# A fused attention and routing kernel: v loaded by heads, two units of filler work moved, and the first k on GpSimd's queue

## The chip, the core and the metric

The kernel runs on one core of a Trainium2 chip. The metric is the device time of one execution in microseconds. Before the change it is 891.77 us, the median of three runs (891.57 to 892.58). One further execution was profiled, and all rows below are of that one.

## What is computed

Two blocks follow each other. The first is an attention without softmax, on four batches of four heads, 1088 positions and 32 values for each position. Each vector of q and k is sent through two small matrices S1 and S2 (8 by 32), and its features are the 64 products of the two results:

```python
def phi(x):
    a = np.einsum('rd,bhsd->bhsr', S1, x)
    b = np.einsum('rd,bhsd->bhsr', S2, x)
    return np.einsum('bhsi,bhsj->bhsij', a, b).reshape(*x.shape[:-1], r * r)
kv = np.einsum('bhsf,bhsd->bhfd', phi(k), v)
z = np.sum(phi(k), axis=2)
num = np.einsum('bhsf,bhfd->bhsd', phi(q), kv)
den = np.einsum('bhsf,bhf->bhs', phi(q), z)[..., None] + 1e-06
```

The result, 4352 rows of 128, is the input x of a dense mixture of eight experts. Logits are `x @ w_gate`; eight rounds of row and column normalisation make weights of them; the output is the sum over the experts of the weight times `relu(x @ w1[e]) @ w2[e]`, with w1 128 by 1024 and w2 1024 by 128.

## The kernel before, in words

Almost all of the arithmetic is the experts' matrix products in float32 on TensorE. The kernel is written so that TensorE can begin them as early as possible. Batch 0 of the attention is worked out first, by itself. From then on there are two streams. One is the attention of batches 1 to 3 and the routing (`attention`, `routing`), which is short on TensorE and waits a great deal for VectorE, ScalarE and DMAs. The other is "filler": products of experts 0 and 1 on the rows of x that are ready, cut into small steps by the generator `steps` (lines L735 for the first product and L797 for the second). Where the attention says `yield n`, the driver calls `fill(n)`, which puts n units of filler on TensorE at that place of the program. TensorE works strictly in the order of the program, so a unit that stands behind a waiting attention product waits too. After the routing the driver drains what is left of the filler, and `weighted` computes everything else (L1076 and L1226, until the end).

The order on TensorE, VectorE and ScalarE is, for the first part, the order of the text. The order on SP, the engine that issues nearly all DMAs, and on GpSimd is made by a scheduler that places each instruction by its own estimate of when it can go. SP issues in that order and waits at the head of it. A DMA also waits for the DMA that is eight places before it on the same queue, since eight semaphores are used in turn.

The names that the steps below touch:

- `load_k`, `load_q`, `load_v` (L169 to L189): one batch of k, q or v into the on-chip memory. k and q come as one DMA of 128 partitions each. v has its positions spread so that partition 32 c + s holds eight positions of block c of row s, for all four heads; it is loaded as four DMAs of 32 partitions (one block c each, all heads) of 128 KB, and two small ones of 32 partitions.
- `projections` (L217 to L225): S1 and S2, which arrive as 64-bit numbers, made into float32 on VectorE (L34 to L47), transposed (`st`, L222) and spread by heads into `wd` (L223). `wd` and the transposed keys `kT` (L269) are what the first real product of TensorE needs (L280).
- `keys_ab`, `keys_products`, `keys_sums` (L280, L295, L310): features of k and their sums with v. `keys_sums(b)` is the reader of v.
- `queries_ab`, `repeat_a`, `repeat_b` (L396 to L423): for batches 1 to 3 the features of q are made through DRAM. Two small products per position (`qab`) are stored to `qa` and `qb` in DRAM, repeated on the way, and read back as `ph` (four DMAs of 288 KB) and `rb` (one of 1152 KB). `times(b, c)` (L430) multiplies them on VectorE, and `tops(b, c)` (L439) multiplies the product with the sums of the keys on TensorE.
- the warming products of ones (L119), six rounds, which keep TensorE at work until the first keys are there.
- the memsets at the beginning, on GpSimd but for three.
- `settle`, `chores_of` (L1327, L1018): inside `weighted`, work on the kept sums of experts 0 and 1: the load of a row of weights (`pk`) and the products with it, put into a list that is worked off at spare places.

Of the kernel before, what the change touches and what calls it, by code (L numbers as in the profile page):

```python
# [10 lines left out]
F32 = mybir.dt.float32  # L11
# [40 lines left out]
def kernel(  # L52
# [12 lines left out]
    nc = tc.nc  # L65
    P = nc.NUM_PARTITIONS
# [36 lines left out]
    for n, (s, queue) in enumerate(((S1, nc.sync), (S2, nc.scalar))):  # L103
        queue.dma_start(out=raw[:, n], in_=s.bitcast(U32).unsqueeze(0).to_broadcast([P // R, R, words * D]))

    def starts(tile_, c0, blocks):

        for c in blocks:
            nc.gpsimd.memset(tile_[32 * c:32 * (c + 1), c0:c0 + 1], 1.0)


    ones = consts.tile([P, P], F32, name="ones")
    nc.gpsimd.memset(ones, 1.0)
    warm = [aps.tile([P, 512], F32, tag="a", name="a") for _ in range(2)]
    for _ in range(6):
        for r in range(2):
            for c in range(2):
                rows, cols = slice(64 * r, 64 * (r + 1)), slice(64 * c, 64 * (c + 1))
                nc.tensor.matmul(warm[r][cols, 0:256], ones[rows, cols], ones[rows, 0:1].to_broadcast([64, 256]),  # L119
                                 start=True, stop=True, tile_position=(64 * r, 64 * c))  # L120
# [28 lines left out]
    kvs = []  # L149
    for i in range(2):  # L150
        kvs.append(consts.tile([P, 2, 2, D + 1], F32, name=f"kvs{i}"))
        nc.gpsimd.memset(kvs[i], 0.0)

    eps = consts.tile([P, 3, H], F32, name="eps")
    nc.gpsimd.memset(eps, 1e-6 / P)

    v_slots = []
    for i in range(2):
        t = wk.tile([P, H + 1, NT + 1, D], F32, name=f"v{i}", bufs=1)
        nc.vector.memset(t[:, H], 1.0)  # L160
        nc.gpsimd.memset(t[H2:P, 0:H, NT], 0.0)
        v_slots.append(t)

    ab = wk.tile([P, 2, NT + 1, H * R], F32, name="ab", bufs=1)
    nc.gpsimd.memset(ab[H2:P, :, NT], 0.0)

    loaded, pools = {}, []

    def load_k(b):  # L169
        kx = ld.tile([P, SA, D], F32, tag="k", name="kx", bufs=1)  # L170
        nc.sync.dma_start(out=kx, in_=k[b].rearrange("h (s a) d -> (h s) a d", a=SA))
        loaded["k", b] = kx

    def load_q(b, lo=0, hi=SA):
        if not lo:
# [3 lines left out]

    def load_v(b):  # L180
        vx, o = v_slots[b % 2], v[b].offset
        for c in range(4):
            nc.sync.dma_start(
                out=vx[32 * c:32 * (c + 1), 0:H, 0:NT, :].rearrange("p h t d -> p h (t d)"),
                in_=AP(tensor=v.tensor, offset=o + NT * D * c, ap=[[SA * D, 32], [S * D, H], [1, NT * D]]))
        for c in range(2):
            nc.sync.dma_start(
                out=vx[32 * c:32 * (c + 1), 0:H, NT, :],
                in_=AP(tensor=v.tensor, offset=o + (4 * NT + c) * D, ap=[[SA * D, 32], [S * D, H], [1, D]]))  # L189

    load_k(0)
    load_q(0, 0, 8)
    load_v(0)
    load_q(0, 8)
# [23 lines left out]
    def projections():  # L218
        flat = raw.rearrange("p n d -> p (n d)")
        s12 = f64_to_f32(nc, consts, flat, (P, 2 * D)) if words == 2 else flat.bitcast(F32)  # L220
        st = consts.tile([P, 2, 32], F32, name="st")
        nc.vector.transpose(out=st.rearrange("p n r -> p (n r)"), in_=s12)  # L222
        nc.vector.tensor_tensor(wd, st[:, :, 0:R].unsqueeze(2).to_broadcast([P, 2, H, R]),  # L223
                                own.unsqueeze(1).unsqueeze(3).to_broadcast([P, 2, H, R]), op=Alu.mult)
        return st  # L225

# [257 lines left out]
    def attention(b):  # L484


        follows = b + 1 < B
        keys_sums(b)
        times(b, 0)
        yield 1.7 if b == 1 else 2  # L490
        keys_kept(b)
        times(b, 1)
        tops(b, 0)
        if b == 1:
            transpose_q(2)
        yield 1.4
        times(b, 2)
        over(b, 0)
        tops(b, 1)
        if b == 1:  # L500
            queries_ab(2)
            repeat_a(2)
        if follows:
            repeat_b(b + 1)
        yield 1.4
        over(b, 1)
        if b + 1 == B:
            take_over(b, 0, 192, nc.gpsimd)
        yield 1.4
        tops(b, 2)  # L510
        if follows:
            transpose_k(b + 1)
        if b + 2 < B:
            load_k(b + 2)
            load_v(b + 2)
        yield 1.4
        over(b, 2)
        if b + 1 < B:
            take_over(b, 0, W9, nc.gpsimd)
        else:  # L520
            take_over(b, 192, W9, nc.sync)
        if follows:
            yield 0.7
            keys_ab(b + 1)
            yield 0.7
            if b == 1:
                transpose_q(3)
            keys_products(b + 1, 0)
            yield 1.4
            keys_products(b + 1, 1)  # L530
            if b == 1:
                queries_ab(3)
                repeat_a(3)
            yield 1.4
            keys_products(b + 1, 2)
            yield 1.4
# [11 lines left out]
    def routing():  # L548

        yield 5  # L550
        for c in range(len(chunks)):
            logits(c)
        yield 1
        for c in range(len(chunks)):
            logits_turned()
        lg = lgp[:, :, 0:E]
        mx = sk.tile([P, 1], F32, tag="mx", name="mx")
        nc.vector.tensor_reduce(out=mx, in_=lg, axis=AX.XY, op=Alu.max)
        yield 3
        pm = bank()[:, 0:P]  # L560
        for s in range(2):
            nc.tensor.matmul(pm[64 * s:64 * (s + 1)], mx.to_broadcast([P, 64]), ident, start=True, stop=True,
                             tile_position=(0, 64 * s))
        nc.vector.reduce_max(mx, pm, axis=AX.X)
        nc.vector.tensor_scalar(mx, mx, -1.0, 64 * math.log(2.0), op0=Alu.mult, op1=Alu.add)
        pw = p2s[0]
        nc.scalar.activation(out=pw[:, :, 0:E], in_=lg, func=Act.Exp, bias=mx[:, 0:1])

        step = 1.5 * 2.0 ** (23 - 149 + 64)
        nc.vector.tensor_scalar(pw[:, :, 0:E], pw[:, :, 0:E], step, step, op0=Alu.add, op1=Alu.subtract)  # L570
        for it in range(ITERS):
            rs = sk.tile([P, SA], F32, tag="rs", name="rs")
            nc.vector.reduce_sum(rs, pw, axis=AX.X)
            nc.vector.reciprocal(rs, rs)
            p1 = p1s[it % 2]
            nc.vector.scalar_tensor_tensor(p1[:, 0:SA], rs.unsqueeze(2).to_broadcast([P, SA, E]), UP,
                                           pw[:, :, 0:E], op0=Alu.mult, op1=Alu.mult)
            cs = sk.tile([P, E], F32, tag="cs", name="cs")
            nc.vector.reduce_sum(cs, p1.rearrange("p g e -> p e g"), axis=AX.X)
            yield 4.25  # L580
            pc = bank()[:, 0:E]
            for s in range(2):
                nc.tensor.matmul(pc[64 * s:64 * (s + 1)], ones[:, 0:64], cs, start=True, stop=True,
                                 tile_position=(0, 64 * s))
            cr = sk.tile([P, E], F32, tag="cr", name="cr")
            nc.vector.reciprocal(cr, pc)
            last = it == ITERS - 1
            pw = lgp if last else p2s[(it + 1) % 2]
            nc.vector.scalar_tensor_tensor(pw[:, :, 0:E], cr.unsqueeze(1).to_broadcast([P, SA, E]),
                                           float(N) / E * (1.0 if last else UP), p1[:, 0:SA],  # L590
                                           op0=Alu.mult, op1=Alu.mult)

        nc.vector.transpose(out=lgT.rearrange("p a s -> p (a s)"), in_=lgp.rearrange("p a e -> p (a e)"))
        for b in (1, 0, 2, 3):
            nc.sync.dma_start(out=pT[:, b * S:(b + 1) * S],
                                                  in_=lgT[32 * b:32 * b + E].rearrange("p a s -> p (a s)"))
# [422 lines left out]
    def chores_of(g):  # L1019
# [10 lines left out]
        def times(o, c):  # L1030
            nc.gpsimd.tensor_tensor(ys[o][:, c], ys[o][:, c], pks[o][:, c], op=Alu.mult)

        chores = []
        for o in range(len(ys)):
            chores += [lambda o=o: load(o), *(lambda o=o, c=c: times(o, c) for c in halves)]
        if len(ys) == 2:
            chores += [lambda c=c: nc.gpsimd.tensor_tensor(ys[0][:, c], ys[0][:, c], ys[1][:, c], op=Alu.add)
                       for c in halves]
        return [(g, do) for do in chores]


    def weighted():
# [283 lines left out]

        def settle(g):  # L1327
            while chores and chores[0][0] <= g:
                do = chores.pop(0)[1]
                leisure.append((lambda engine, do=do: do(), True))  # L1330

        def plus(out_, x, y, op=Alu.add):
            leisure.append((lambda engine: engine.tensor_tensor(out_, x, y, op=op), True))
# [217 lines left out]
```

## Time and profile before

| | |
|---|---|
| median of three runs | 891.77 us |
| the profiled execution's own time | 894.25 us |
| its span, first to last instruction | 892.5 us |
| mean granted clock of TensorE | 0.999 |
| DMA over the span | 179.10 MB, mean 201 GB/s |
| VectorE busy | 764.8 us (86%) |
| ScalarE busy | 544.8 us (61%) |
| GpSimd busy | 276.4 us (31%) |

The profiled execution took 1.75 us more than its span, and 2.48 us more than the median of the runs that were not profiled. In the rows, PE is TensorE's matrix products and PEld its weight loads, DVE is VectorE, ACT ScalarE, POOL GpSimd, and SPq the queue of SP. A row of a timeline has the start, the duration, the engine, the line of the kernel, the operation, what it writes and reads, the shape and the count; in brackets stands how long the engine was idle before it and what ended that. A row of DMA issues has the transfer, the issuing queue, the count, the size of each and the median time from issue to landing. "DMA share" is the mean busy share of the core's 16 DMA engines.

### The profile page before, as it was taken

How to read it: one execution, taken by the hardware profiler on the slowest of the kernel's cores; microseconds unless marked ns; L12 is line 12 of the kernel's file. 1: busy time of each engine (PE TensorE's matmuls, PEld its weight loads, DVE VectorE, ACT ScalarE, POOL GpSimd, SP SyncE). 2: the span in 40 equal slices, each digit the busy share in tenths (PEclk: the TensorE clock that was granted, in tenths of full speed). 3: DMA queues.
4: the chain of work that ended last, by engine and by line, in shares of the span. 5: the costliest groups of instructions: out<-in, count | busy, mean ns of one | idle time of the engine just before them, and what ended most of it. 6: DMA issues, size and time to landing. Idle time of an engine off the chain costs nothing.

```text
span 892.5 us, 36433 instructions
## 1 busy us (share of the span) xinstructions
PE 881.5 (99%) x15308; PEld 634.6 (71%) x15308; DVE 764.8 (86%) x1338; ACT 544.8 (61%) x1086; POOL 276.4 (31%) x317
## 2 busy tenths in 40 slices
PE   9899999999999999999999999999999999999997
PEld 6678544547667767777777776777877799877875
DVE  8589689978998988888888888888899889889986
ACT  3346456645666666666666666666666666666664
POOL 3121125464552223233213312322333222332311
PEclk9999999999999999999999999999999999999999
DMA  8999399886785866477567666665774874774861
GB/s 230 277 287 253 91 236 259 115 242 196 240 258 166 241 197 206 126 223 218 170 172 205 203 174 191 211 172 161 219 245 132 264 219 145 230 245 134 244 198 28
DMA packets 146419, 179.10 MB, mean 201 GB/s; under 512 B 55984, under 2 KB 93568, under 8 KB 145872
## 3 DMA queue, kind: packets, MB, share of 16 engines
q1 hardware_dynamic: 138624, 166.67, 64.7%
q0 software_dynamic: 6528, 9.95, 5.8%
q8 instruction: 121, 1.98, 0.9%
q14 instruction: 42, 0.34, 0.1%
q10 hardware_dynamic: 1104, 0.15, 0.1%
HBM read 134.22 MB, written 25.99 MB: 180 GB/s over the span
## 4 chain that ended last, share of the span: by engine, by line
PE 96%; DVE 1%; DMA 1%; issue 1%; ACT 0%; SPq 0%; POOLq 0%; POOL 0%; DVEq 0%; ACTq 0%
PE pair L1076 39%; PE s L1226 38%; PE a L735 9%; PE s L797 7%; PE a L310 1%; PE a L439 1%; DMA kx<-in_k_dram 1%; PE a L280 0%; DMA w<-z 0%; PE s L349 0%; PE s L369 0%; DVE hb L750 0%; PE a L403 0%; PE a L473 0%; DVE ph L360 0%
## 5 line engine op out<-in xcount | busy, mean ns | idle before, releaser
L1076 PE MATMUL pair<-xf,w1x 64*64 64x256 f32 (+1 forms) x6736 | 502.1, 366 | 0.1
L1076 PEld LDWEIGHTS pair<-xf,w1x 64*64 64x64 f32 x6736 | 260.0, 133 | 91.5 <-DVE hb L1086 6.8
L1086 DVE TENSOR_TENSOR hb<-pair,copies 128x512 f32<-128x512 f32 (+1 forms) x354 | 233.5, 662 | 64.7 <-ACT xf L1099 24.3
L1226 PE MATMUL s<-hb,w 64*64 64x256 f32 (+1 forms) x3824 | 286.6, 365 | 0.0
L1226 PE MATMUL s<-hb,ws 64*64 64x256 f32 (+1 forms) x2848 | 213.4, 365 | 0.0
L1089 ACT ACTIVATE hb<-hb 128x512 f32<-128x512 f32 (+1 forms) x238 | 144.4, 608 | 103.8 <-DVE hb L1086 98.4
L1226 PEld LDWEIGHTS s<-hb,w 64*64 64x64 f32 x3824 | 151.5, 133 | 47.5 <-issue 0.3
L1005 POOL TENSOR_TENSOR xf<-xT,pb 128x512 f32<-128x512 f32 (+1 forms) x60 | 75.0, 1251 | 254.1 <-ACT xf L1099 213.7
L1013 POOL TENSOR_TENSOR xf<-xf 128x512 f32<-128x512 f32 (+1 forms) x59 | 72.3, 1225 | 214.1 <-ACT xf L1099 139.4
L1226 PEld LDWEIGHTS s<-hb,ws 64*64 64x64 f32 x2848 | 112.8, 133 | 35.0
L735 PE MATMUL a<-xT,w 128*64 128x416 f32 (+3 forms) x512 | 119.0, 465 | 0.0
L737 ACT ACTIVATE hb<-a 128x416 f32<-128x416 f32 (+3 forms) x128 | 59.7, 469 | 66.3 <-PE a L735 55.6
L1089 ACT ACTIVATE hb<-pair 128x512 f32<-128x512 f32 (+1 forms) x126 | 72.5, 575 | 44.1 <-PE pair L1076 43.8
L1133 DVE SCALAR_TENSOR_TENSOR hb<-hb 128x512 f32<-128x512 f32 (+1 forms) x118 | 80.8, 685 | 16.0 <-ACT hb L1089 3.9
L1163 ACT COPY copies<-pair 128x512 f32<-128x512 f32 (+1 forms) x118 | 66.5, 564 | 30.7 <-PE pair L1076 30.7
L1160 ACT COPY copies<-pair 128x512 f32<-128x512 f32 (+1 forms) x118 | 66.5, 563 | 30.3 <-PE pair L1076 30.3
L1156 ACT COPY copies<-pair 128x512 f32<-128x512 f32 (+1 forms) x118 | 66.6, 564 | 26.4 <-PE pair L1076 26.4
L1136 DVE TENSOR_TENSOR hb<-hb 128x512 f32<-128x512 f32 (+1 forms) x118 | 79.0, 669 | 3.0 <-DVE xf L1015 0.2
L1138 DVE TENSOR_TENSOR hb<-hb 128x512 f32<-128x512 f32 (+1 forms) x118 | 81.2, 688 | 0.0
L1137 DVE SCALAR_TENSOR_TENSOR hb<-hb 128x512 f32<-128x512 f32 (+1 forms) x118 | 80.1, 678 | 0.0
L750 DVE TENSOR_TENSOR hb<-hb 128x416 f32<-128x416 f32 (+7 forms) x84 | 61.0, 727 | 14.8 <-ACT hb L737 6.8
L797 PE MATMUL s<-hb,ws 128*64 128x416 f32 (+3 forms) x224 | 71.3, 474 | 0.7 <-DVE hb L750 0.7
(191 smaller groups left out, 675.9 us busy)
## 6 DMA issues: line engine op xcount, KB each, us to landing
w1x<-w1x SPq DMA_DIRECT2D x135, 256.0 KB, 4.1
w<-w2x SPq DMA_DIRECT2D x103, 256.0 KB, 4.1
ws<-w2x SPq DMA_DIRECT2D x51, 256.0 KB, 3.9
pb<-pT SPq DMA_DIRECT2D x35, 256.0 KB, 4.3
xf<-xf SPq DMA_DIRECT2D x70, 128.0 KB, 2.8
ws<-w2x SPq DMA_DIRECT2D x52, 128.0 KB, 3.8
w1x<-w1x SPq DMA_DIRECT2D x7, 896.0 KB, 5.6
w1x<-w1x SPq DMA_DIRECT2D x45, 128.0 KB, 4.0
```

Source lines behind the costliest of these rows:

```text
L735: nc.tensor.matmul(ph[sl], loaded_w[j][0][:, P * f + H2 * s:P * f + H2 * (s + 1)], xT[:, at + lo:at + hi], start=True, stop=True, tile_pos ...
L797: nc.tensor.matmul(sums[g][i][H2 * s:H2 * (s + 1)], w, x, start=c == 1, stop=c == per, tile_position=(0, H2 * s))
L1005: nc.gpsimd.tensor_tensor(xf[:, 0:2].rearrange("p b n -> p (b n)"), xT[:, lo:lo + 2 * n], weights.pop(i), op=Alu.mult)
L1013: nc.gpsimd.tensor_tensor(xf[:, 4:6], xf[:, 1:4:2], xf[:, 0:2], op=Alu.subtract)
L1076: nc.tensor.matmul(out[H2 * col:H2 * (col + 1), r], w1[rows, PLACE[form], o:o + H2], xf[rows, x], start=start, stop=stop, tile_position=(H ...
L1086: nc.vector.tensor_tensor(flat(out, n), x, flat(y, n), op=Alu.add)
L1089: nc.scalar.activation(out=x, in_=y, func=Act.Relu)
L1133: nc.vector.scalar_tensor_tensor(ts[:, 0], h[:, 3], 0.0, h[:, 0], op0=Alu.max, op1=Alu.subtract)
L1136: nc.vector.tensor_tensor(ts[:, 2], h[:, 1], ts[:, 0], op=Alu.subtract)
L1137: nc.vector.scalar_tensor_tensor(ts[:, 1], h[:, 3], 0.0, h[:, 1], op0=Alu.max, op1=Alu.subtract)
L1138: nc.vector.tensor_tensor(ts[:, 3], h[:, 2], ts[:, 2], op=Alu.subtract)
L1226: yield lambda rho=rho, rows=rows, c=c: nc.tensor.matmul(acc[g][rho][q][H2 * half:H2 * (half + 1), n * place:n * (place + 1)], w[rows], fl ...
```

## The change

Seven edits, in the order of the diff:

1. The load of batch 0's k is issued by GpSimd, as its first work, in place of SP, where it was second.
2. `ones`, `kvs`, `eps` and the zeroed ends of `v` and `ab` are set by VectorE, not GpSimd.
3. Five rounds of warming products, not six.
4. `load_v` loads by heads: four DMAs of one head each, 128 KB, over all 128 partitions. The source of each is four blocks of 32 rows of 1 KB.
5. `wd` is made on GpSimd, behind `st`.
6. In the attention of batch 1 the first `yield` is 3.7 units in place of 1.7; two yields of the routing become 0.6 and 3.4 in place of 1 and 3. The sum over a whole run stays, since what is left is drained at the end of the routing.
7. In `weighted`, the loads of `pk` of a group are issued at once when the group is settled; the products with them stay in the list.

```diff
+    load_k(0, nc.gpsimd)
...
-    nc.gpsimd.memset(ones, 1.0)
+    nc.vector.memset(ones, 1.0)
...
-    for _ in range(6):
+    for _ in range(5):
...
-        nc.gpsimd.memset(kvs[i], 0.0)
+        nc.vector.memset(kvs[i], 0.0)
...
-    nc.gpsimd.memset(eps, 1e-6 / P)
+    nc.vector.memset(eps, 1e-6 / P)
...
-        nc.gpsimd.memset(t[H2:P, 0:H, NT], 0.0)
+        nc.vector.memset(t[H2:P, 0:H, NT], 0.0)
...
-    nc.gpsimd.memset(ab[H2:P, :, NT], 0.0)
+    nc.vector.memset(ab[H2:P, :, NT], 0.0)
...
-        for c in range(4):
+        for h in range(H):
             nc.sync.dma_start(
-                out=vx[32 * c:32 * (c + 1), 0:H, 0:NT, :].rearrange("p h t d -> p h (t d)"),
-                in_=AP(tensor=v.tensor, offset=o + NT * D * c, ap=[[SA * D, 32], [S * D, H], [1, NT * D]]))
+                out=vx[:, h, 0:NT, :].rearrange("p t d -> p (t d)"),
+                in_=AP(tensor=v.tensor, offset=o + S * D * h, ap=[[NT * D, 4], [SA * D, 32], [1, NT * D]]))
...
-    load_k(0)
     load_q(0, 0, 8)
...
-        nc.vector.tensor_tensor(wd, st[:, :, 0:R].unsqueeze(2).to_broadcast([P, 2, H, R]),
+        nc.gpsimd.tensor_tensor(wd, st[:, :, 0:R].unsqueeze(2).to_broadcast([P, 2, H, R]),
...
-        yield 1.7 if b == 1 else 2
+        yield 3.7 if b == 1 else 2
...
-        yield 1
+        yield 0.6
...
-        yield 3
+        yield 3.4
...
-        chores = []
-        for o in range(len(ys)):
-            chores += [lambda o=o: load(o), *(lambda o=o, c=c: times(o, c) for c in halves)]
+        chores = [lambda o=o: load(o) for o in range(len(ys))]
+        chores += [lambda o=o, c=c: times(o, c) for o in range(len(ys)) for c in halves]
...
-                do = chores.pop(0)[1]
-                leisure.append((lambda engine, do=do: do(), True))
+                _, do, at_once = chores.pop(0)
+                if at_once:
+                    do()
+                else:
+                    leisure.append((lambda engine, do=do: do(), True))
```

The built program of the changed kernel shows one more thing, which the diff alone does not: the scheduler gives SP another order. Before, the stores and loads of batch 1's query features (`qa`, `qb`, `ph`, `rb`) stand directly behind batch 1's v. After the change these stand between them:

```
w1 (expert 1)  128x1024
w2 (expert 1)  128x8x128
v0 (batch 2)   128x1x256 x2
qx (batch 2)   128x1088
v0 (batch 2)   128x1x256 x2
v0 (batch 2)   32x4x32
qa1, qb1 x2, ph1 x4, rb     (batch 1)
```

Before, all of these loads stood behind `rb`; the last small piece of batch 2's v still does.

More of the change, by code (lines that the diff above doesn't have):

```diff
@@ L104, with load_k @@
         queue.dma_start(out=raw[:, n], in_=s.bitcast(U32).unsqueeze(0).to_broadcast([P // R, R, words * D]))
+    loaded = {}
+    def load_k(b, queue=nc.sync):
+        kx = ld.tile([P, SA, D], F32, tag="k", name="kx", bufs=1)
+        queue.dma_start(out=kx, in_=k[b].rearrange("h (s a) d -> (h s) a d", a=SA))
+        loaded["k", b] = kx
+    load_k(0, nc.gpsimd)
     def starts(tile_, c0, blocks):
@@ L160 @@
         nc.vector.memset(t[:, H], 1.0)
-        nc.gpsimd.memset(t[H2:P, 0:H, NT], 0.0)
+        nc.vector.memset(t[H2:P, 0:H, NT], 0.0)
         v_slots.append(t)
     ab = wk.tile([P, 2, NT + 1, H * R], F32, name="ab", bufs=1)
[L165 to L172, printed above, removed]
+    nc.vector.memset(ab[H2:P, :, NT], 0.0)
     def load_q(b, lo=0, hi=SA):
@@ L1038, in chores_of @@
                        for c in halves]
-        return [(g, do) for do in chores]
+        return [(g, do, i < len(ys)) for i, do in enumerate(chores)]
     def weighted():
```

## The prediction

> **What bounds the kernel now.** I read the busy times of the page first, then the waits of TensorE, then the timelines around them, and last the DMA queue of SP.
>
> ```profile
> span 892.5 us, 36433 instructions
> PE 881.5 (99%) x15308; PEld 634.6 (71%) x15308; DVE 764.8 (86%) x1338; ACT 544.8 (61%) x1086; POOL 276.4 (31%) x317
> 300.00:892.50 592.50, 587.44 (x11516) 445.32 (x11508) 515.51 (x912) 380.70 (x732) 169.22 (x173) 1.00 0.65 190
> ```
>
> TensorE is busy 99% of the span, and from 300 us on (third row, a stage of the table by stretches: length, then PE) it lacks 592.50 − 587.44 = 5.1 us, nearly all of it the end, after its last product. The change leaves the products alone, so it can only close idle time of TensorE or open some. The idle places before 300 us:
>
> ```profile
> 0.99 5.40 PE L119 MATMUL a<-ones 64*64 64x256 f32 x48 [0.99 <-POOL own L122]
> 6.98 1.28 PE L280 MATMUL a<-wd,kT 128*64 128x64 f32 x32 [0.58 <-DVE kT L269]
> 9.44 2.48 PE L310 MATMUL a<-v,kp 128*64 128x64 f32 x72
> 34.62 0.60 PE L797 MATMUL s<-hb,w 128*64 128x256 f32 x4
> 37.80 0.92 PE L439 MATMUL a<-kvs,ph 128*64 128x66 f32 x24 [2.58 <-issue]
> 68.23 0.39 PE L439 MATMUL a<-kvs,ph 128*64 128x66 f32 x6 [0.82 <-issue]
> 36.64 1.83 DVE L430 TENSOR_TENSOR ph<-ph,rb 128x768 f32<-128x768 f32 x2 [7.17 <-DMA rb<-qb]
> ```
>
> Two matter. Real work begins at 6.98, when the first keys are turned. And at 35.22 the filler is used up: TensorE stands 2.58 us in front of `tops(1, 0)`. The bracket says "issue", but the last row tells who is late: VectorE, which makes its operand, waited for the DMA of `rb` until 36.64, and TensorE went on 37.80 − 36.64 = 1.16 us later. The time of that first `tops` is therefore set by one DMA chain. Its issues on SP and times to landing:
>
> ```profile
> 1.50 0.81 SPq L171 DMA_DIRECT2D kx<-in_k_dram  x1
> 2.83 1.85 SPq L183 DMA_DIRECT2D v<-in_v_dram  x4
> 9.59 3.86 SPq L183 DMA_DIRECT2D v<-in_v_dram  x4
> 18.11 0.63 SPq L410 DMA_DIRECT2D qa<-qab  x1
> 22.96 3.98 SPq L420 DMA_DIRECT2D ph<-qa  x4
> 27.12 0.44 SPq L423 DMA_DIRECT2D rb<-qb  x1
> 27.61 0.43 SPq L178 DMA_DIRECT2D qx<-in_q_dram  x1
> 30.46 7.87 SPq L183 DMA_DIRECT2D v<-in_v_dram  x4
> qa<-qab SPq DMA_DIRECT2D x1, 144.0 KB, 4.0
> rb<-qb SPq DMA_DIRECT2D x1, 1152.0 KB, 9.4
> ```
>
> `qa` goes out at 18.11 and lands at 22.1; `rb` goes out at 27.12 and lands at 36.5. How fast the queues work in these stretches (length, five engines' busy time, granted clock, DMA share, GB/s):
>
> ```profile
> 16.00:19.00 3.00, 2.92 (x32) 1.88 (x30) 2.99 (x7) 1.72 (x5) 0.60 (x1) 1.00 1.12 166
> 20.00:27.00 7.00, 7.00 (x83) 5.13 (x81) 5.86 (x12) 4.35 (x12) 3.10 (x5) 1.00 0.97 249
> 34.00:38.00 4.00, 1.42 (x18) 0.73 (x16) 1.36 (x2) 1.14 (x3) 0.00 (x0) 1.00 0.99 399
> 40.00:43.00 3.00, 3.00 (x54) 2.69 (x51) 1.80 (x4) 1.11 (x3) 0.00 (x0) 1.00 1.12 147
> 174.00:177.00 3.00, 3.00 (x20) 1.59 (x18) 2.85 (x5) 2.94 (x8) 0.00 (x0) 1.00 0.31 46
> ```
>
> All 16 DMA engines are occupied in the first four, so `rb` lands late because bytes stand ahead of it. With v loads in flight (16 to 19, 40 to 43) they move only 147 to 166 GB/s, with whole rows of k, q and weights (34 to 38) 399, or 25 per engine, in the mixed stretch 249, or 15.6.
>
> **The change part by part.**
>
> *The start (k first on GpSimd, memsets, `wd`, five rounds).* What these free, with the rows:
>
> ```profile
> 3.18 0.48 DVE L34 TENSOR_SCALAR bits<-raw 128x64 uint32<-128x64 uint32 x1 [1.43 <-DMA raw<-in_S_dram]
> 5.21 0.24 DVE L222 STREAM_TRANSPOSE st<-s 128x64 f32<-128x64 f32 x1
> 5.56 0.35 DVE L223 TENSOR_TENSOR wd<-st,own 128x64 f32<-128x64 f32 x1
> 6.21 1.30 DVE L269 STREAM_TRANSPOSE kT<-kx 128x512 f32<-128x512 f32 x2 [0.30 <-DMA kx<-in_k_dram]
> 0.74 0.20 POOL L113 MEMSET ones<- 128x128 f32 x1 [0.29 <-POOLq L1535]
> 2.18 0.36 POOL L152 MEMSET kvs<- 128x132 f32 x2
> 2.47 0.12 POOL L155 MEMSET eps<- 128x12 f32 x1
> 2.65 0.34 POOL L161 MEMSET v<- 64x128 f32 x2
> 2.93 0.15 POOL L165 MEMSET ab<- 64x64 f32 x1
> 18.40 0.72 POOL L410 DMA_DIRECT2D qa<-qab  x1 [11.22 <-ACT qab L406]
> qa<-qab POOLq DMA_DIRECT2D x1, 144.0 KB, 3.9
> ```
>
> k goes out at 0.74 in place of 1.50, and a DMA of GpSimd lands as soon after its issue as one of SP (3.9 against 4.0 for `qa`). The seven memsets that move to VectorE, 0.20 + 0.36 + 0.12 + 0.34 + 0.15 = 1.2 us by the GpSimd rows, fit into its 1.43 us of waiting for `raw`; without that cover they would cost 1.2 us. `wd` on GpSimd has only the products `wq` and `wdq` behind it, whose readers (L349, L403) come after the keys. With `wd` gone, `kT` can begin behind `st`, at about 5.5 in place of 6.21. So TensorE may start its real work up to 0.7 us earlier; the warming, 5.40 × 5/6 = 4.5 us, still ends before that. Bounds: 0 to 0.7 us gained.
>
> *v by heads.* The amount is the same, 512 KB in four DMAs. What it costs depends on how a DMA is dealt to the 16 engines. Before, both sides' outermost step had 32 places. Now the destination has 128 partitions, but the source's outermost step has four. One end: dealt over all 16, at the 399 GB/s of 34 to 38, a set takes 1.3 us, against 512 KB at 147 to 166 GB/s = 3.2 to 3.6 now. Other end: dealt by that step of four, on four engines, 128 KB per engine at 25 GB/s each, or at 20, halfway to the 15.6, = 5.2 to 6.5 us, and every later DMA that uses all 16 waits for these four. The nearest row is the store of the routing weights, the only DMAs at 174 to 177: their outer step has eight places, and the share is 0.31 and the rate 46 GB/s, as if no more than half of the engines had work. I take four engines. The Trainium skill ("DMA: Bandwidth & Descriptors", section "Why a DMA increments its semaphore by 16 and not by 1") speaks against the change in the same sense: a copy runs on the largest number of engines, up to 16, that divides the outermost sizes of both sides, here four of 128 and 4. No run here shows a 128 against 4 yet; by it the upper end holds, without it the sum would be that of the first rival.
>
> *The new order on SP.* Ahead of batch 1's `qa` now stand two weight loads (512 KB each), q of batch 2 (544 KB) and batch 2's v. q alone also holds SP until the last of q of batch 0 is turned, when `qa` was already out at 18.11:
>
> ```profile
> 19.01 0.43 DVE L264 STREAM_TRANSPOSE qT<-qx 128x288 f32<-128x288 f32 x1
> ```
>
> That is 19.4, and the issues behind it follow, so it binds only if the queues themselves are fast.
>
> The sum for the landing of `rb`, from 36.5:
> - weights and q: 1568 KB / 16 = 98 KB per engine, at 25 to 15.6 GB/s: + 3.9 to + 6.3.
> - v: three sets ahead in place of two: 3 × (5.2 to 6.5) − 2 × 3.4 = + 8.8 to + 12.7.
> - the earlier k: 0 to − 0.7.
> - while the four busy engines are the bound, the other traffic on them (k, q and weights of the first two batches and the additions, about 350 KB per engine) may run at 25 in place of 20 GB/s: 17.5 − 14 = 3.5, so 0 to − 3.5.
>
> That is 36.5 + 8.5 = 45.0 to 36.5 + 19.0 = 55.5. I take + 11.3 (4.5 + 9.5 − 0.7 − 2, somewhat nearer to the fast ends, whose rate the trace holds for 4 us), so `rb` lands at 47.8, and `tops(1, 0)` starts at 47.8 + 1.3 = 49.1.
>
> *The two units.* They put three more pairs of filler in front of `tops(1, 0)`, six in place of three. A pair takes
>
> ```profile
> 38.62 0.71 PE L735 MATMUL a<-xT,w 128*64 128x288 f32 x4
> 39.56 0.69 PE L735 MATMUL a<-xT,w 128*64 128x288 f32 x4
> ```
>
> 39.56 − 38.62 = 0.94 us, so 2.8 us. If `rb` were no later, they would fill the hole of 2.58. They are work that is done anyway, so at `tops(1, 0)` the kernel is behind by 49.1 − 37.80 − 2.8 = **8.5 us** (from the two ends: 5.7 to 16.2). TensorE reaches that place at 35.2 + 2.8 = 38, give or take the 0.7 gained or the 2 to 3 us by which the first v may now hold up L310; either is swallowed, as it is before 45. Everything behind on TensorE, VectorE and ScalarE is queued in order and shifts with it.
>
> *Later.* The hole of 0.82 at 67.4 may close, as the weights and q that competed there are now early: 0 to − 0.8, I take − 0.3. The pk loads that go earlier take up to 1.0 us of SP's queue each:
>
> ```profile
> 288.73 1.00 SPq L1028 DMA_DIRECT2D pk<-pT  x1
> ```
>
> TensorE shows no wait for a load behind them in the 592 us, so I count 0; without that cover a weight load would be late by 1.0 us at each. The two routing yields cancel.
>
> Sum + 8.2: the profiled kind of execution goes from 894.25 to 902.5, and the median, 2.48 lower, from 891.77 to **900.0 us**. For a hole of this length the Trainium skill ("TensorE: Matmul & The Clock Gate", section "HAM oscillation — how this bites in real kernels") would add something: after an idle window of about 3.4 us the clock falls to half for as long again, an estimate of + 1.7 us. The trace does not show it, as its longest hole, 2.58 us, left the clock at 1.00.
>
> **The rivals.**
> 1. *All 16 engines serve v.* Then v costs 3 × 1.3 − 2 × 3.4 = − 2.9, and the order on SP + 3.9 to 6.3, − 0.7 for k: `rb` lands 0.3 to 2.7 later, at 36.8 to 39.2, and the kernel is ahead by 39.3 less that, 2.5 to 0.1; with SP held by q until 19.4 and four more issues of 0.45 (`qa` 3 us late) it is behind by up to 1. Time 889.3 to 892.8, say 891.0. For it: the load does go to 128 partitions. Against it: four blocks in the source.
> 2. *Faster: `rb` in time.* As rival 1, and the stores that GpSimd issues (half of `qa` and `qb`) run ahead during the wait, so `rb` lands by 36.0 and TensorE, arriving at 37.3, no longer stands. Then 2.58 + 0.7 is gained: 888.5. It decides at a landing of 37.3 − 1.3 = 36.0. Against it: 1568 KB more ahead of `rb`.
> 3. *Four engines, but partly hidden*: SP runs far enough ahead that the other twelve finish early, and `rb` lands near 41: + 1.7, 893.5.
>
> **How the numbers follow.** The forecast 0.66, with 896.7 to 908 as its own range (5.7 − 0.8 to 16.2); rival 1 0.18, rival 2 0.11, rival 3 0.05. For 8 times in 10 the range must reach to rival 1: 889.5 to 906, which leaves out most of rival 2 and the upper end. A measurement can tell 0.2%, 1.8 us, so "same" is 890.0 to 893.6. Slower 0.66 + 0.03 + 0.01 = 0.70 (the forecast and parts of rivals 3 and 1); faster 0.11 + 0.04 = 0.15 (rival 2 and a part of 1); same 0.15.
>
> **What would show it.** After: k turned by about 5.6 and L280 near 6.2; L310 held up by v past 10; v's stretches at 70 to 110 GB/s with a DMA share near a quarter once nothing else is queued; `qa` out after 25, `rb` landing after 44, and a hole of 6 us or more in front of the first L439. It is wrong if the four v DMAs land within 2 us of each other's start at over 250 GB/s, or if SP sends `qa` before 22.

## The result and the profile after

The changed kernel takes **905.76 us** in the median (905.24 to 907.43, five runs), the kernel before on the same chip 891.57 (890.32 to 892.58). The ratio is 1.0163, 95% interval 1.0148 to 1.0178: slower by 1.6%. The profiled execution took 907.43 us, 13.18 more than that of before.

The page of the changed kernel: span, busy times, and the clock in 40 slices of 22.6 us.

```profile
span 905.6 us, 36417 instructions
PE 886.0 (98%) x15300; PEld 656.2 (72%) x15300; DVE 763.7 (84%) x1345; ACT 544.8 (60%) x1086; POOL 274.5 (30%) x311
PEclk9979999999999999999999999999999999999999
```

TensorE now lacks 19.6 us of the span, and it is busy 4.5 us longer although one round of ones is gone, mostly because the clock fell, most of all in the third slice. Where it stands is in the timelines of TensorE and VectorE (start, duration; in brackets the idle time before and what ended it):

```profile
5.68 1.30 DVE L270 STREAM_TRANSPOSE kT<-kx 128x512 f32<-128x512 f32 x2 [0.15 <-DMA kx<-in_k_dram]
6.54 1.19 PE L281 MATMUL a<-wd,kT 128*64 128x64 f32 x32 [0.94 <-DVE kT L270]
11.19 0.33 PE L311 MATMUL a<-v,kp 128*64 128x64 f32 x2 [1.48 <-DMA v<-in_v_dram]
13.22 3.44 PE L311 MATMUL a<-v,kp 128*64 128x64 f32 x66 [1.70 <-DMA v<-in_v_dram]
42.08 0.60 PE L798 MATMUL s<-hb,w 128*64 128x256 f32 x4
50.74 1.83 DVE L431 TENSOR_TENSOR ph<-ph,rb 128x768 f32<-128x768 f32 x2 [16.38 <-DMA rb<-qb]
51.80 1.59 PE L440 MATMUL a<-kvs,ph 128*64 128x66 f32 x24 [9.12 <-DMA v<-in_v_dram]
53.33 1.23 PE L736 MATMUL a<-xT,w 128*64 128x288 f32 x4
55.18 1.20 PE L736 MATMUL a<-xT,w 128*64 128x288 f32 x4
58.68 1.19 PE L404 MATMUL a<-qT,wdq 128*64 128x192 f32 x12
```

The keys are turned at 5.68, when k lands, 0.16 us behind `st`. Then batch 0's v, which used to be in time, holds up L311 twice, and in front of the first L440 (L439 of before) there is a hole of 9.12 us in place of 2.58. The bracket names v, but the row above says what it is: VectorE waits for `rb` until 50.74, 14.1 us later than before. The pairs behind the hole are 1.85 us apart (53.33 to 55.18), where 0.92 is usual. The issues of SP and GpSimd, from their timelines, say why `rb` is late:

```profile
2.35 2.41 SPq L185 DMA_DIRECT2D v<-in_v_dram  x4
13.63 5.53 SPq L185 DMA_DIRECT2D v<-in_v_dram  x4
19.20 1.51 SPq L189 DMA_DIRECT2D v<-in_v_dram  x2
21.76 5.68 SPq L185 DMA_DIRECT2D v<-in_v_dram  x2
23.11 0.57 POOL L411 DMA_DIRECT2D qa<-qab  x1 [15.60 <-ACT qab L407]
28.10 3.33 SPq L185 DMA_DIRECT2D v<-in_v_dram  x2
32.73 0.65 SPq L411 DMA_DIRECT2D qa<-qab  x1
39.61 2.58 SPq L421 DMA_DIRECT2D ph<-qa  x4
42.38 0.44 SPq L424 DMA_DIRECT2D rb<-qb  x1
```

Before, SP was done with batch 1's v at 14.66, where it is now at 20.71:

```profile
13.49 1.17 SPq L187 DMA_DIRECT2D v<-in_v_dram  x2
```

The first four v DMAs take 0.6 us each to issue. The third set takes 5.68 for two and 3.33 for two: SP stands in the issue itself, though the DMA eight places before each of them had landed. So it comes to `qa` at 32.73, although GpSimd issued its half of `qa` at 23.11, when the operand was ready. And `ph` waits until 39.61 for that `qa`, because `qa`'s bytes stand behind v: by the trace's semaphore records twelve of its 16 updates came by 36.64, the other four, as many as v has engines, from 38.35 to 39.53. The stretches show how the DMA engines and the clock fare (length, five engines' busy time, clock, DMA share, GB/s):

```profile
6.00:7.00 1.00, 0.46 (x15) 0.49 (x16) 1.00 (x3) 0.00 (x0) 1.00 (x5) 1.00 0.30 85
44.00:46.00 2.00, 0.00 (x0) 0.00 (x0) 0.00 (x0) 0.00 (x0) 0.00 (x0) 1.00 0.96 330
46.00:48.00 2.00, 0.00 (x0) 0.00 (x0) 0.00 (x0) 0.00 (x0) 0.00 (x0) 0.68 0.90 303
52.00:54.00 2.00, 2.00 (x32) 1.78 (x32) 2.00 (x3) 0.00 (x0) 0.00 (x0) 0.50 0.35 120
54.00:56.00 2.00, 2.00 (x12) 1.16 (x10) 1.93 (x4) 0.41 (x1) 0.00 (x0) 0.50 0.35 103
56.00:58.00 2.00, 2.00 (x18) 1.25 (x16) 1.57 (x4) 0.66 (x2) 0.00 (x0) 0.76 0.15 45
```

From 6 to 7 hardly anything but v is under way, and the share is 0.30 at 85 GB/s: about a quarter of the engines work. The trace's semaphore records agree. A v DMA leaves five updates, one right after its issue and four with the data; a load of k or q leaves 16. The Trainium skill ("DMA: Bandwidth & Descriptors", section "Why a DMA increments its semaphore by 16 and not by 1") says that only the engines which take part post an update and that the issuing sequencer writes the rest at once; this trace agrees, with four.

**Where 13.2 us went.** L440 begins 51.80 − 37.80 = 14.0 us later, with three more pairs (2.75 us) ahead of it: 11.25. From there to the first product of the last part,

```profile
193.35 0.45 PE L1076 MATMUL pair<-xf,w1x 64*64 64x256 f32 x4
```

before and

```profile
206.79 0.45 PE L1076 MATMUL pair<-xf,w1x 64*64 64x256 f32 x4
```

after, TensorE loses another 13.44 − 11.25 = 2.2, the halved clock less some small holes. The rest of the span is 0.3 shorter: 0.9 longer in some 690 us of products, 1.2 shorter after the last one. These small remainders are of one execution each; the kernel before, profiled a second time (e9), had a span 2.0 us shorter.

### The profile page after: what moved, and what is told of

Same layout as the page of the kernel before. It is cut to its first block, busy times and chain, and to the rows that moved or that the text cites. A ratio compares the mean times of both kernels' runs of the same rounds, so it can differ in the third digit from the quotient of the medians.

```text
span 905.6 us, 36417 instructions
## 1 busy us (share of the span) xinstructions
PE 886.0 (98%) x15300; PEld 656.2 (72%) x15300; DVE 763.7 (84%) x1345; ACT 544.8 (60%) x1086; POOL 274.5 (30%) x311
## 4 chain that ended last, share of the span: by engine, by line
PE 94%; DMA 2%; DVE 2%; SPq 1%; ACT 0%; issue 0%; DVEq 0%; ACTq 0%
PE pair L1076 38%; PE s L1226 38%; PE a L736 8%; PE s L798 6%; DMA v<-in_v_dram 1%; PE a L311 1%; PE a L440 1%; DMA qa<-qab 1%; SPq L185 1%; DVE hb L751 1%; PE s L370 0%; PE a L281 0%; PE s L1242 0%; SPq L421 0%; PE a L404 0%
## 5 line engine op out<-in xcount | busy, mean ns | idle before, releaser
L736 PE MATMUL a<-xT,w 128*64 128x416 f32 (+3 forms) x512 | 123.7, 470 | 0.4 <-DVE kT L483 0.4
L751 DVE TENSOR_TENSOR hb<-hb 128x416 f32<-128x416 f32 (+7 forms) x84 | 56.9, 680 | 18.5 <-ACT hb L738 15.4
```

The costliest lines, as they stand in the source:

```text
L736: nc.tensor.matmul(ph[sl], loaded_w[j][0][:, P * f + H2 * s:P * f + H2 * (s + 1)], xT[:, at + lo:at + hi], start=True, stop=True, tile_pos ...
```

## The experiments

Two theories stood against each other. **D**: each v DMA now runs on four engines, and everything that uses all 16 waits behind it. **O**: it is the new order on SP, with weights, q and a third v set ahead of `qa`. Ratios are against the kernel before, run on the same chip (its medians there were 892.0 to 893.0), with 95% intervals. For each the row of VectorE's first product with `rb` says when `rb` was there.

### e1: the same order, 16 engines

```diff
-                in_=AP(tensor=v.tensor, offset=o + S * D * h, ap=[[NT * D, 4], [SA * D, 32], [1, NT * D]]))
+                in_=AP(tensor=v.tensor, offset=o + S * D * h, ap=[[SA * D, 32], [NT * D, 4], [1, NT * D]]))
...
-            nc.vector.transpose(out=kT[:, 0:NT * P].rearrange("p (t c s) -> p c t s", c=4, s=32)[:, :, lo:hi],
+            nc.vector.transpose(out=kT[:, 0:NT * P].rearrange("p (t s c) -> p c t s", c=4, s=32)[:, :, lo:hi],
```

> The changed kernel with one thing altered: the positions of a block of v are dealt to the partitions as 4 s + c in place of 32 c + s (the transposed keys are written in the same order), so that the source's outermost step has 32 places in place of 4. The same four DMAs by head, of the same bytes, in the same order on SP. Theory D (the dealing: four DMA engines carry v, and all else queues behind them): each v DMA gets 17 semaphore updates in place of 5, a set lands within 2.5 us of its first issue when little is queued, L311 of batch 0 is not held up, rb lands at 36 to 40 in place of 50.6, the hole in front of the first L440 is under 3 us; 889 to 893 us, I say 890.5. Theory O (the new order on SP, with weights, q and batch 2's v ahead of qa, is the cause by itself): qa still goes out after 28, the hole stays over 5 us: 898 to 906.

Measured: 894.51 us, ratio 1.0029 (1.0014 to 1.0044). Timeline of e1:

```profile
9.14 4.76 SPq L185 DMA_DIRECT2D v<-in_v_dram  x4
24.97 0.65 SPq L411 DMA_DIRECT2D qa<-qab  x1
40.22 1.83 DVE L431 TENSOR_TENSOR ph<-ph,rb 128x768 f32<-128x768 f32 x2 [9.66 <-DMA rb<-qb]
41.27 0.92 PE L440 MATMUL a<-kvs,ph 128*64 128x66 f32 x24 [3.20 <-issue]
```

With the two outer steps of the source swapped (and the keys written in the same order), and not one DMA more, fewer or earlier in the queue, `rb` comes 10.5 us sooner. Each v DMA leaves 16 updates (not the 17 of the expectation), batch 0's last v DMA lands at 7.5 in place of 13.2, L311 is no longer held up, and SP issues the second set from 9.14 in place of 13.63. That is what D gave: in this order of SP, four fifths of the loss hang on the number of engines. What is left is slightly above what D gave (889 to 893): a hole of 3.20 us, and behind it a clock of 0.50 from 42.5 to 45.9, which the expectation did not have.

### e2: four engines, the order of before

Each early DMA of SP (k, q, v, weights, `ph`, `rb`) is put into one order, as here for `rb`:

```diff
-        nc.sync.dma_start(out=rb, in_=queries.pop(b)[1].rearrange("h i (j x) s n -> (h i j) x (s n)", x=2))
+        tc.keep_in_program_order(nc.sync.dma_start(out=rb, in_=queries.pop(b)[1].rearrange("h i (j x) s n -> (h i j) x (s n)", x=2)))
```

> The changed kernel, with SP's early DMAs held to the order of the text, which is the order of the kernel before (batch 1's qa, qb, ph and rb ahead of q of batch 2, expert 1's weights and batch 2's v). v still goes by heads, with four engines. Theory D alone (the engines occupied by v decide, whatever the order): rb lands after 44, 898 to 906. Theory O: qa goes out at 23 to 25, as soon as its operand is there, rb lands at 34 to 40, which is before TensorE comes to the first L440 at 42.7; no hole there. The hold of L311 at 10 to 13 and the halved clock behind it (together 4.7 us by the changed kernel's trace) stay and now count: 891.6 + 4.7 - 2.6 - 0.4 = 893.3, range 891 to 897. I hold that both are needed for the hole of 9 us, so I expect this one, 893.3.

Measured: 895.34 us, ratio 1.0037 (1.0020 to 1.0053). Timeline of e2:

```profile
13.37 3.66 PE L311 MATMUL a<-v,kp 128*64 128x64 f32 x66 [1.65 <-DMA v<-in_v_dram]
23.19 0.67 SPq L411 DMA_DIRECT2D qa<-qab  x1
39.94 1.83 DVE L431 TENSOR_TENSOR ph<-ph,rb 128x768 f32<-128x768 f32 x2 [5.39 <-DMA rb<-qb]
42.88 0.87 PE L440 MATMUL a<-kvs,ph 128*64 128x66 f32 x24
```

`qa` goes out 9.5 us sooner than in the changed kernel, `rb` is there 10.8 us sooner, and TensorE, itself late by the hold of L311, no longer waits at L440. The 3.3 us that remain are more than the 1.7 that I named, but inside the range; they are that hold and a start whose products take twice their time (last section). So the order alone undoes as much as the engines alone: neither theory by itself is right.

### e3 and e4: both undone

e3 has `load_v` of before (and with it, from the scheduler, SP's order of before) and all else of the change. e4 has the edits of e1 and e2 together.

> The changed kernel with v loaded as before, in four DMAs by block of 32 partitions (the order on SP then is that of before by itself). It keeps the start (k on GpSimd, memsets and wd moved, five rounds of ones) and the two units. Theories D and O agree here: the loss goes, and what is left is the start (0 to 0.5 us gained) and the hole of 2.58 filled by 2.8 us of pairs: 888.5 to 891, I say 889.3. If the start or the two units had a share in the loss (theory S), it stays above 892.5.

> Both undone: v by heads on partitions 4 s + c (32 places outermost) and SP's early DMAs held to the order of the kernel before. Theory D: as e1 or up to 1 us better, 888 to 890.5, I say 889; rb lands at 32 to 36, no hole over 1 us in front of the first L440. Theory O: the same. If 128-partition loads of 1 KB rows are no faster than 32-partition ones of the same rows, it equals e3.

Measured: e3 890.83 us, ratio 0.9989 (0.9976 to 1.0002); e4 892.40 us, 1.0010 (0.9996 to 1.0023). In both `rb` is in time and L440 has no hole. Timeline rows of e3 and e4:

```profile
18.16 0.63 SPq L411 DMA_DIRECT2D qa<-qab  x1
33.62 1.83 DVE L431 TENSOR_TENSOR ph<-ph,rb 128x768 f32<-128x768 f32 x2 [4.09 <-DMA rb<-qb]
```

```profile
6.96 0.69 PE L281 MATMUL a<-wd,kT 128*64 128x64 f32 x16 [1.76 <-DVE kT L270]
8.85 2.08 PE L350 MATMUL s<-qT,wq 64*128 64x256 f32 x8
35.81 1.83 DVE L431 TENSOR_TENSOR ph<-ph,rb 128x768 f32<-128x768 f32 x2 [4.51 <-DMA rb<-qb]
```

So the start and the two units have no share in the loss: theory S is out. The four cases as a table, `rb` ready at:

| | order of before | new order |
|---|---|---|
| v on 16 engines | 35.81 (e4) | 40.22 (e1) |
| v on 4 engines | 39.94 (e2) | 50.74 (the change) |

Each factor costs about 4 us alone and 10 to 11 us on top of the other. Single profiles scatter here: e8 and e11, which differ only in yields far behind this place, have `rb` at 33.62 and 35.80, so the 10 is clear and the 4 is rough. In time the ratios say the same: against e4, e1 loses 1.7 us and e2 2.4, the change 13.6, since TensorE has filler until 38 to 43 us and a `rb` that comes by then costs nothing.

The 4 us of the four engines alone are not spent in the queue. e2 has the order of e3, but SP sends `qa` at 23.19 in place of 18.16, as soon as its operand is there: TensorE, held at L311 for batch 0's v, makes that operand 5.0 us later. From `qa` to `rb` the two take nearly the same, 16.75 and 15.46 us. With the new order, SP itself is late at `qa`, and the more so the slower v is: 24.97 in e1, 32.73 in the change. I read it so that SP's order and the engines are one queue, where what stands ahead is as dear as the engines are slow; no run here varies the two in finer steps.

e4 came out 2 us above its range: the products of its start take twice their time (L350: 2.08 us here, 1.14 in the kernel before), see e8.

### e5: the hole filled with products of ones

```diff
         times(b, 1)
+        if b == 1:
+            extra = [bank() for _ in range(2)]
+            for n in range(76):
+                r, c = n % 2, n // 2 % 2
+                rows, cols = slice(64 * r, 64 * (r + 1)), slice(64 * c, 64 * (c + 1))
+                nc.tensor.matmul(extra[r][cols, 0:256], ones[rows, cols], ones[rows, 0:1].to_broadcast([64, 256]),
+                                 start=True, stop=True, tile_position=(64 * r, 64 * c))
         tops(b, 0)
```

> The changed kernel with 76 products of ones put on TensorE in front of the first L440 (8.6 us of work by the 0.113 us that one of the warming products takes), so that the hole of 9.12 us is filled with work that nobody reads. rb lands as late as before, at 50.6, and the first L440 begins at 51.8 either way. Theory C (the idle time also costs the clock afterwards, 0.50 from 47 to 57): the clock stays at 1.00, the pairs behind take 0.92 in place of 1.8, 2.6 us less than the changed kernel: 1.0134 of the kernel before. Rival (the halved clock costs nothing that counts, since DMAs or VectorE set the pace there): 1.016, as the changed kernel.

Measured: 905.92 us, ratio 1.0139 (1.0116 to 1.0162). That interval alone does not decide between 1.0134 and 1.016. The timeline of e5 does:

```profile
44.13 8.50 PE L499 MATMUL a<-ones 64*64 64x256 f32 x152
52.56 0.92 PE L440 MATMUL a<-kvs,ph 128*64 128x66 f32 x24
56.97 1.18 PE L404 MATMUL a<-qT,wdq 128*64 128x192 f32 x12
```

(The profile counts two for each of these products.) From L440 to L404 the same products take 4.41 us here and 58.68 − 51.80 = 6.88 in the changed kernel, whose clock was at 0.50. The idle time cost 2.5 us beyond itself. 0.8 of it is not seen in the sum, as L440 began 0.8 later here.

### e6: the kernel before, with v by heads only

> The kernel before with v by heads (source with four places outermost) and nothing else of the change. On SP, expert 1's weights and q of batch 2 now stand ahead of batch 1's qa, but batch 2's v stands behind rb. So two v sets on four engines are ahead of rb, not three. Theory D: L310 of batch 0 is held to about 13 (+ 4.7 on TensorE), qa goes out at 22 to 25, rb lands at 40 to 44, the first L439 begins at 41.5 to 45.5 in place of 37.8: + 3.7 to + 7.7, and up to 2 more if the clock falls: 895 to 901, I say 898. If v's form by itself were the whole cause: + 14 and more, as TensorE has 2.8 us less filler ahead of the hole: 905 to 909. If it were the start or the two units: no change.

Measured: 903.54 us, ratio 1.0115 (1.0093 to 1.0136): + 10.3, more than expected. Timeline of e6:

```profile
25.25 3.90 SPq L414 DMA_DIRECT2D qb<-qab  x2
34.54 2.78 SPq L420 DMA_DIRECT2D ph<-qa  x4
45.83 1.83 DVE L430 TENSOR_TENSOR ph<-ph,rb 128x768 f32<-128x768 f32 x2 [11.26 <-DMA rb<-qb]
46.99 1.59 PE L439 MATMUL a<-kvs,ph 128*64 128x66 f32 x24 [6.68 <-issue]
```

SP was on time with `qa` here (23.20), but the bytes of `qa` stood behind two v sets, w1, q and w2 and landed at 34.5; `ph` could not be issued before. So `rb` is ready at 45.83 with two v sets ahead, against 39.94 in e2, which has no weights and q ahead, and 50.74 in the change, which has a third set. v by heads alone, with the order that the scheduler makes of it, explains most of the loss without any of the other edits.

### e7 and e9: the two units, and the hole of the kernel before

e7 changes the three yields of the kernel before (3.7, 0.6, 3.4), nothing else; e9 is the kernel before, profiled again.

> The kernel before with the two units moved (first yield 3.7 in place of 1.7, in the routing 0.6 and 3.4) and nothing else. SP's order of the first 60 us stays. Filler of 2.8 us goes into the hole of 2.58 in front of the first L439, so that one closes: - 2.6, to 889 (range 888 to 890.5), ratio 0.997. If another wait takes its place (batch 2's keys or q): no change, ratio 1.000. In e3, which has the start's edits besides, the ratio was 0.9989, so I expect 0.998 to 0.999 here.

> The kernel before, unaltered, profiled once more. The first profile of it (894.25 us, 2.5 us above the median) shows a hole of 2.58 us in front of the first L439, and e7, which fills that hole with the two units, came out only 0.5 us faster in the median. Theory V (the hole was larger in the profiled execution than it mostly is): here the landing of rb is earlier than 36.5 and the hole under 2 us, with a span of 889 to 891. Rival (the hole is always there, and e7 loses its 2.6 us elsewhere): again 2.3 to 2.8 us, with rb at 36 to 37.

Measured: e7 891.71 us, ratio 0.9992 (0.9980 to 1.0005); e9 892.26 us in its one run, span 890.5. The first L439 in e7 and in e9:

```profile
37.74 0.87 PE L439 MATMUL a<-kvs,ph 128*64 128x66 f32 x24
```

```profile
37.41 0.92 PE L439 MATMUL a<-kvs,ph 128*64 128x66 f32 x24 [2.42 <-issue]
```

Theory V falls: the hole is there again, 2.42 us. In e7 it is gone, and the span is 1.4 us shorter than e9's, not 2.4: a hole of 0.43 us stands in front of a filler product at 113 us, which the kernel before does not have, and the rest is not tracked. A gain of 1.4 us lies inside the interval of the ratio, so the units are worth about 0.1%, if anything.

### e8: e4 with six rounds of ones

> As e4 (v by heads on partitions 4 s + c, SP's early DMAs in the order of the kernel before), with six rounds of ones again in place of five. In e4 TensorE stood 1.76 us between the ones and the first keys and the clock was at 0.50 from 8 to 11. Theory C: with 0.9 us more of ones the clock stays at 1.00 there, which gives back 1.5 us: ratio to the kernel before 0.9995 or less, e4 had 1.001. If the loss of e4 comes from the slower transposes alone (2.0 in place of 1.3 us for L270), it stays at 1.001.

Measured: 891.56 us, ratio 0.9987 (0.9974 to 1.0000), against e4's 1.0010. Timeline of e8:

```profile
6.78 0.69 PE L281 MATMUL a<-wd,kT 128*64 128x64 f32 x16 [1.32 <-DVE kT L270]
8.34 1.13 PE L350 MATMUL s<-qT,wq 64*128 64x256 f32 x8
```

The same products run at full speed, and batch 0's L311 begins at 9.41 in place of 10.86: 1.45 us, what theory C gave. The transposes are as slow as in e4.

### e10: only the weights behind rb

```diff
-        nc.sync.dma_start(out=w1, in_=moe_w1[e])
+        tc.keep_in_program_order(nc.sync.dma_start(out=w1, in_=moe_w1[e]))
...
-        nc.sync.dma_start(out=w2, in_=moe_w2[e].rearrange("(fo fi) d -> fi fo d", fi=P))
+        tc.keep_in_program_order(nc.sync.dma_start(out=w2, in_=moe_w2[e].rearrange("(fo fi) d -> fi fo d", fi=P)))
```

> The changed kernel, with the loads of the experts' weights alone held to the order of the text on SP: expert 1's w1 and w2 (1024 KB) go behind rb, while the third v set and q of batch 2 stay ahead of batch 1's qa. Theory D, with SP as the place (SP stands because each v DMA finds the four engines' queues full): qa still goes out after 28, as the v DMAs of the third set take 1.3 us and more each to issue; rb lands at 46 to 48.5, which is 64 KB per engine at 15.6 to 25 GB/s = 2.6 to 4.1 us earlier than in the changed kernel; the hole is 4 to 7 us; ratio 1.011 to 1.014. If the weights' bytes were the main term of the order, rb would land before 43 and the ratio be under 1.008.

Measured: 903.14 us, ratio 1.0107 (1.0087 to 1.0128). Timeline of e10:

```profile
20.91 4.34 SPq L185 DMA_DIRECT2D v<-in_v_dram  x4
28.39 0.65 SPq L411 DMA_DIRECT2D qa<-qab  x1
47.40 1.83 DVE L431 TENSOR_TENSOR ph<-ph,rb 128x768 f32<-128x768 f32 x2 [12.98 <-DMA v<-in_v_dram]
48.46 1.59 PE L440 MATMUL a<-kvs,ph 128*64 128x66 f32 x24 [5.54 <-DVE ph L431]
```

`qa` still goes out after 28, and `rb` is ready 3.3 us sooner, inside the 2.6 to 4.1. The 1024 KB of weights are worth 3.3 us, not the main term. The ratio is just below the 1.011 to 1.014 expected: by the ratios this kernel is 5.0 us faster than the changed one, and what the 1.7 us beyond `rb` are was not followed; its runs lie from 900.4 to 904.6.

### e11 and e12: a version that beats both

Both are the changed kernel with six rounds of ones and the routing's yields of before; e11 has v as in e4, e12 as in the kernel before.

> A version meant to beat both kernels: the changed kernel with v by heads on partitions 4 s + c (16 engines), SP's early DMAs in the order of the kernel before, six rounds of ones, and the routing's yields as before (1 and 3). It is e8 without the routing part of the moved units. In e8 and the other kernels with that part a hole of 0.43 us stands at 113 to 130 in front of a filler product, which the kernel before does not have. Theory: that hole goes, and the hole in front of the first L440 stays closed: 0.4 us better than e8, ratio 0.998. If another wait of the routing comes back in its place (before: 0.65 us at 188): 0.9987, as e8.

> The changed kernel with v loaded as before (blocks of 32 partitions; SP's order is then that of before by itself), six rounds of ones and the routing's yields as before. It keeps k on GpSimd, wd and the memsets, the filler ahead of the first L440 and the early pk loads. Expected as e3 (0.9989) less 0.4 us: 0.9985. Against e11 it tells whether the form of v with 16 engines is worth anything once the order on SP is that of before: theory D says no (rb is in time for TensorE either way), a difference of under 0.1%.

Measured: e11 891.61 us, ratio 0.9980 (0.9967 to 0.9993); e12 890.72 us, **0.9977** (0.9965 to 0.9989). Both are faster than the kernel before, by 0.2%, and than the changed one by 1.8%. The form of v is worth nothing there that could be measured, as D said: 0.0003 lies between them. The hole of 0.43 us at 113 is still in e11 and not in e12, so the routing's yields are not its cause; what is stays open.

## Why the prediction was too low

The sign, the place and the cause (four engines for v, more loads ahead of `qa`) were right. The size was not: the sum that gave it had one term too small and one left out. 900.0 was forecast, 905.76 measured, a loss of 8.2 us forecast and, in the profiled executions, 13.2 found. By the ratio it lies at 906.3 on the scale of the 891.77 shown, just above the 906.0 of the range. The medians differ by 14.2, as the profiled execution of before lay 2.68 us above its median and that of the change 1.67; the balance here is that of the profiled pair.

- *v by heads on four engines*: right. 85 GB/s and a share of 0.30 where v is alone, 21 GB/s per engine, inside the 20 to 25 assumed; e1 shows that it is the number of engines. Rivals 2 and 3, with `rb` by 36.0 and near 41, are out by its 50.74.
- *The sum for `rb`*: the step that failed. It said 47.8; VectorE had it at 50.74 and the first L440 came at 51.80 in place of 49.1, 2.7 us more. The sum added up the bytes per DMA engine that stand ahead of `rb`. For v, weights and q it added 14.0 (4.5 + 9.5) and took 2.7 off. By the rows all that was added stands in front of `qa`'s landing, and there it was 17.4: 39.53 in place of 22.1. From there to `rb` the chain, with less queued ahead of it, took 11.2 us in place of 14.5, so a relief of 3.3 us came. 17.4 − 3.3 is the 14.1 measured, where 14.0 − 2.7 gave 11.3.
  What the added term had not counted is the place on SP. The prediction let SP be held by q until 19.4 and said that this binds only with fast queues. In fact SP issued `qa` 32.73 − 18.11 = 14.6 us later, and it was SP itself that came late. Up to the end of batch 1's v it was 6 us behind: three times it waited for a v DMA of batch 0 to land, 3.9 us in all by the view of its waits, and it stood in the second set. Weights, q and the third set took it another 11.9 us, to 32.64; only the 3.4 us that it used to wait for `qab` came off. Once issued, `qa` took 6.8 us to land in place of 4.0, its last four updates behind v.
  The hold of L310 (now L311), which the prediction gave 2 to 3 us, was 4.7 (done at 16.66 in place of 11.92), and as `qab` is made behind it, GpSimd's half of `qa` went out 4.7 us later, at 23.11. In the change SP's lateness covers that, so "swallowed" held; in e2 and e6, where SP is in time, `qa` goes out by it.
  Split into v, weights and q the 14.1 cannot be: without the weights `rb` came 3.3 us sooner (e10), with no third set 4.9 (e6, which differs in the start and the units too), and single profiles scatter by 2 us.
- *The clock*: the other failed step. The sum left it out, since the trace of before had no hole beyond 2.58 us. e5 measures it at 2.5 us, and 2.2 stand in the balance. 8.2 + 2.7 + 2.2 = 13.1 us, against 13.2; that it closes so well is chance, as two profiles of the kernel before differ by 2 us. The rule of the Trainium skill ("TensorE: Matmul & The Clock Gate", section "What's actually happening") that the prediction quotes, with an estimate of + 1.7, speaks in the right sense; this kernel's runs make it somewhat dearer.
- *The new order on SP*: right that it counts, and more than thought: with v on 16 engines it alone brings `rb` from 35.81 to 40.22, which is above the first rival's 36.8 to 39.2, and that rival's time (889.3 to 892.8) was missed by e1 because of it and of the clock behind its hole.
- *The two units*: 2.8 us as counted; they filled the hole in e7.
- *The start*: k was to go out at 0.74 and went out at 1.28; L281 began at 6.54 in place of 6.98. In e3, with the same start and v as before, L281 began at 7.04, and the start of the kernel before gave 6.61 in e7 and 6.75 in e9: no gain can be told from the scatter.
- *Later*: the hole of 0.82 closed, that of 0.66 too; but e9, the kernel before, has no hole of 0.82 either. The end after the last product was 1.2 us shorter, which was counted as 0. No experiment followed that.

## What to carry to other kernels

In these runs the outermost step of the source decided how many engines carry a DMA (four updates with data for a step of 4, sixteen for one of 32): load the same bytes with the long step outside, and look at the DMA share where that transfer is alone. A slow DMA is not only late itself. Here the engine that issues waited for it and stood in it, up to 2.8 us in one issue, and its reader held TensorE, so that the operand of a later store was 4.7 us late; and an order that cost 1.7 us with fast loads became the bound. So follow when each store and load of a chain can be issued, and not only how many bytes stand ahead of the last. And if a hole of 3 us or more is forecast for TensorE, a halved clock for some 5 us behind it belongs in the sum.

## What was not expected of the hardware

**The clock comes late and stays.** The rows of the clock give, for the four holes above 3 us, when it fell and when it was back:

| kernel | hole from | length | clock down from | TensorE at work from | clock back at |
|---|---|---|---|---|---|
| the change | 42.7 | 9.1 | 46.7 | 51.8 | 57.0 |
| e10 | 42.9 | 5.5 | 47.2 | 48.5 | 54.0 |
| e6 | 40.3 | 6.7 | 44.8 | 47.0 | 51.6 |
| e1 | 38.1 | 3.2 | 42.5 | 41.3 | 45.9 |

(The edges are worked out from the mean clock of stretches of 1 or 2 us, as if it were 1.00 or 0.50.) It fell 4.0 to 4.5 us after the hole began, in e1 after TensorE was back at work, and returned 4.6 to 5.6 us after the work did, whatever the length. The clock was down for 10.3, 6.8, 6.8 and 3.4 us: about three times, twice and once 3.4, as if it were set anew at steps of that length. Holes of 2.58 and 2.42 us did nothing. Idle time in pieces counts as well: 1.48 and 1.70 us in front of L311, with 0.3 us of work between, brought 0.50 from 12.6 to 16 in the changed kernel.

**Five rounds of ones are at the edge.** With five and a wait of 1.33 us (e2) or 1.76 us (e4) behind them the first products ran at half speed (L350: 2.08 us); with five and 0.94 to 1.44 us (the change, e1, e3) they did not, nor in any kernel with six. The length of the wait alone does not decide: 1.33 us halved the speed, 1.44 did not. In e2 the row of the clock says 1.00 in that stretch, but its trace has no record of the clock before 16.6 us; the durations tell.

**A transpose that writes every fourth place is slower**: L270 took 2.0 us for its two halves in e1 and e4, 1.30 with places side by side.
